# Fewer warming matmuls, a hand-made front order and a split first unit in a spectral-filter and token-mixing kernel

## The chip, the cores and the metric

The kernel runs on one core of one Trainium2 chip. The metric is the device time of one execution in microseconds (us). Beside it stands the span of the profile, from the first to the last instruction, which is shorter: by 1.5 to 1.6 us in every recorded run of the kernel before and of e2, and by 1.75 to 1.9 us in every run of the changed kernel and its other edits. So the changed kernel spends some 0.26 us more outside its span; no run here tells where. "Granted clock" is the share of full speed that TensorE was allowed; it was 0.995 or more in all runs compared below, except where the text says otherwise.

## The reference

A batch of 1 with 2048 tokens of 512 channels is normalized, filtered in the frequency domain, added to itself, normalized again, and mixed along the tokens by a two-layer network.

```python
h  = x + irfft2(rfft2(layernorm(x)) * (w_r + 1j * w_i))   # over tokens and channels
u  = gelu(einsum("bsd,sf->bdf", layernorm(h), w1) + b1)   # F = 1376
h2 = h + transpose(einsum("bdf,fs->bds", u, w2) + b2)
```

Inputs, weights and the output are bf16.

## The kernel before

Every operation is recorded by name (`f2_3_01`, `hh_4`) with the engine it runs on and two numbers in ns: `occ`, how long it keeps its engine, and `lat`, when its result is there. A list scheduler then fixes the order of each engine's program *before anything runs*, always taking the operation that could start first by those numbers. The chip executes each engine's list strictly in that order. So these numbers don't merely describe the program, they shape it.

```python
def act(name, dst, src, func, n, ...):                 # every ScalarE operation
    lat = 186.0 + 0.833 * n + 93.0 * naps + (93.0 if accum is not None else 0.0)
    ...
    return K.op(name, "act", emit, ins=ii, outs=oo, occ=lat - 90.0, lat=lat + 50.0, ...)
...
# schedule(): of all operations that are ready
st = max(eng_free[o.stream], o.dep_ready, avail, o.not_before)
key = (st, -o.prio, o.idx)                             # the smallest key goes next
...
eng_free[e] = st + o.occ
```

The front: 16 tiles of tokens. Statistics of a tile on VectorE (ScalarE for tiles 1 and 3), its reciprocal root on ScalarE, a scaling FS of the transform's matrix, matmuls, an evacuation Y. Some matmuls of zeros ("warming") keep TensorE busy meanwhile.

```python
STAT_ACT = (1, 3)
FS_ENG = {4: "act", 7: "act", 9: "dve", 11: "dve", 13: "dve", 14: "act", 15: "dve"}   # others GpSimd
N_WARM = 20
WARM_AFTER = (4, 3, 2, 1, 1, 0, 1, 0, 0, 0, 0, 0, 0, 0, 0, 0)
```

The middle: 8 units. Per unit two groups of second-transform matmuls (f2, full rows, 256 columns), an evacuation CS for each, cross matmuls (x, on 64 rows each), VectorE's product with the spectral weights, 16 matmuls back (g1, full rows, 128 columns) and an evacuation PQ.

```python
def stage_f2(u):
    for i in range(2):
        G = 2 * u + i
        ...  # 4 matmuls f2_G into one bank
        # CS of G on ScalarE (VectorE for G == 1)
def stage_x(u):
    ...      # 8 matmuls x_2u, x_2u+1 into two banks, half=True (64 rows)
    ...      # one product of 128 x 2048, or two of 1024 for units in V_SPLIT = (0, 7)
def stage_g1(u):
    ...      # twice 8 matmuls and an evacuation PQ on ScalarE
for u in range(8):
    stage_f2(u); stage_x(u); stage_g1(u)
```

After that, per tile: inverse transform (g2, `eo` on ScalarE, g3), the residual on VectorE (`tl`, `th`, `h`), the sum of squares and its root on ScalarE (`q`, `r2`), and the normalized tile on VectorE (`hh`). Each `hh` feeds the first layer of the network on TensorE.

```python
    act(f"eo_{s2}", EO[:, s2, :], lambda bank: ps[:, bank, :], ACT.Copy, 512, ...)
    ...  # tl, th, h on VectorE
    act(f"q_{s2}", junk()[:, :], hs, ACT.Square, 512, ..., accum=V2[:, s2:s2 + 1], prio=9)
    act(f"r2_{s2}", R2[:, s2:s2 + 1], V2[:, s2:s2 + 1], ACT.Abs_reciprocal_sqrt, 1, ...)
    dve(f"hh_{s2}", ...)                               # HH = (h + nm) * r2
```

Of the kernel before, what the change touches and what calls it, by code (L numbers as in the profile page):

```python
# [8 lines left out]
LN_EPS = 1e-5  # L9
# [27 lines left out]
def _row(sign, comp, k2, s):  # L37
    return 4 * (k2 * 2 + s) + 2 * sign + comp
# [52 lines left out]
def build_consts():  # L91
# [22 lines left out]
    fp = fp.reshape(NP, NS2, NP)  # L114
    fp = np.stack([-fp, fp], axis=2)
# [26 lines left out]
    c["E"] = e.reshape(NP, 1024)  # L142
    c["MR"] = np.concatenate([m.reshape(NP, 512), r.reshape(NP, 512)], axis=1)
# [5 lines left out]
PSUM_BANKS = 8  # L149
CELL = 4  # L150
# [28 lines left out]
class Builder:  # L179
    def __init__(self, nc, limits):  # L180
        self.nc = nc
        self.ops = []
        self.writer = {}
        self.readers = {}
        self.tensors = {}
        self.limits = limits
        self.cell_cache = {}

# [37 lines left out]
    def op(self, name, engine, emit, ins=(), outs=(), occ=100.0, lat=None, unit=None, pr=False, pw=False,  # L226
           first=False, last=False, prio=0, nbytes=0, is_dma=False, not_before=0.0, after=(), group=None, rate=DMA_RATE):
# [13 lines left out]
        o.rate = rate  # L241
        deps = {id(d): d for d in after}
# [38 lines left out]
    def schedule(self):  # L281
# [13 lines left out]
        order = []  # L295
        while len(order) < len(ops):
            best = None
            for o in ready:
                bank, avail = None, 0.0
                u = o.unit  # L300
                if u is not None and not u.claimed:
# [5 lines left out]
                    for b in range(PSUM_BANKS - u.nbanks + 1):  # L307
                        if all(bank_unit[i] is None for i in range(b, b + u.nbanks)):
                            t = max(bank_free[b:b + u.nbanks])
                            if cand is None or t < cand[0]:  # L310
                                cand = (t, b)
# [10 lines left out]
            ready.remove(o)  # L322
            o.sched, o.start = True, st
# [11 lines left out]
            if o.is_dma:  # L335
                x0 = max(st + (3200.0 if st < 4000.0 else 1700.0), dma_free)
                dma_free = x0 + o.bytes / o.rate
                o.finish = dma_free + 200.0
            else:
                o.finish = st + o.lat  # L340
# [86 lines left out]
def memory_layout():  # L427
# [26 lines left out]
    add("W", [NP, NG, 2, LW], bf, rw)  # L454
    add("HH", [NP, NS2, D_LEN], bf, rw)
# [28 lines left out]
STAT_ACT = (1, 3)  # L484
RS_GROUPS = ((0,), (2,), (4,), (5,), (6, 7), (8, 9), (10, 11), (12,), (13,), (14,), (15,))
FS_ENG = {4: "act", 7: "act", 9: "dve", 11: "dve", 13: "dve", 14: "act", 15: "dve"}
Y_DVE = ((5, 1), (6, 1), (7, 1))
N_WARM = 20
WARM_AFTER = (4, 3, 2, 1, 1, 0, 1, 0, 0, 0, 0, 0, 0, 0, 0, 0)
V_SPLIT = (0, 7)  # L490
LAST_WARM = 6
# [3 lines left out]
def build_kernel(nc, A_x, A_w_r, A_w_i, B_w1, B_b1, B_w2, B_b2, out):  # L495
# [5 lines left out]
    K = Builder(nc, {"f1": 6, "f2": 2, "x": 2, "g1": 2, "g2": 2, "g3": 2, "mm1": 5, "mm1b": 6, "mm2": 8})  # L501
# [3 lines left out]
    X, FS, Y, CS, V, PQ, EO, H, HH, GT, OUT, W = (T[n] for n in ("X", "FS", "Y", "CS", "V", "PQ", "EO", "H", "HH", "GT", "OUT", "W"))  # L505
# [9 lines left out]
    def dma(name, dst, src, nbytes, stream="sp", outs=(), ins=(), prio=0, strided=False, after=(), group=None, rate=DMA_RATE,  # L515
            not_before=0.0):
        def emit(eng, bank):
            if strided:
                with nc.allow_non_contiguous_dma(reason="small bias gather"):
# [3 lines left out]
                    rate=rate, occ=1000.0 if stream == "pool" else 640.0 if rate < DMA_RATE else 460.0, not_before=not_before)  # L523
# [10 lines left out]
    def act(name, dst, src, func, n, ins=(), outs=None, unit=None, prio=0, last=True, psum=True, bias=None, scale=None, accum=None):  # L534
# [15 lines left out]
        return K.op(name, "act", emit, ins=ii, outs=oo, occ=lat - 90.0, lat=lat + 50.0, unit=unit, pr=unit is not None,  # L550
# [13 lines left out]
    def ldf(q, pr_, stream="sp", nb=0.0):  # L564
        sl = slice(4 * q, 4 * q + 4)
        dma(f"ld_FP{q}", FP[:, sl, :, :], cin[f"FP{q}"][:, :, :, :], 1 << 18, outs=[FP[:, sl, :, :]], prio=pr_, stream=stream, not_before=nb)

    for q, (a, b) in enumerate(((0, 2), (2, 4), (4, 6), (6, 8), (8, 12))):
        ldx(a, b, 90 - q)
    ldf(2, 84)  # L570
    ldx(12, 16, 83)
    ldf(3, 82)
    ldf(0, 90, "act")
    act("table", T["tb"][:, 0:1], EPS[:, 0:1], ACT.Abs_reciprocal_sqrt, 1, ins=[EPS[:, 0:1]], prio=88)
    ldf(1, 87, "act", 1800.0)
    dma("ld_E", EM[:, 0:1024], cin["E"][:, :], 1 << 18, outs=[EM[:, 0:1024]], prio=44)
    dma("ld_MR", EM[:, 1024:2048], cin["MR"][:, :], 1 << 18, outs=[EM[:, 1024:2048]], prio=43)
    wload = {}
    for ch, (u0, u1) in enumerate(((0, 1), (1, 4), (4, 8))):
        g0, ng = 4 * u0, 4 * (u1 - u0)  # L580
        lst = []
        for w, dram in ((0, A_w_r), (1, A_w_i)):
            for comp in range(2):
                d = W[comp::4, g0:g0 + ng, w, :]
                lst.append(dma(f"ld_wp{ch}_{w}{comp}", d, bass.AP(dram.tensor, g0 * LW, [[64 * LW, 32], [LW, ng], [1, LW]]),
                               32 * ng * 514, prio=42 - ch, group=f"w{ch}", rate=300.0))
                h0, nh = (g0, ng) if g0 else (1, ng - 1)
                d = W[2 + comp::4, h0:h0 + nh, w, :]
                lst.append(dma(f"ld_wm{ch}_{w}{comp}", d, bass.AP(dram.tensor, (64 - h0) * LW, [[64 * LW, 32], [-LW, nh], [1, LW]]),
                               32 * nh * 514, prio=42 - ch, group=f"w{ch}", rate=300.0))  # L590
                if g0 == 0:
                    d = W[2 + comp::4, 0, w, :]
                    lst.append(dma(f"ld_wz{ch}_{w}{comp}", d, bass.AP(dram.tensor, 32 * LW, [[64 * LW, 32], [1, LW]]),
                                   32 * 514, prio=42 - ch, group=f"w{ch}", rate=300.0))
        for u in range(u0, u1):
            wload[u] = lst
    dma("ld_D2", EM[:, 2048:3072], cin["D2"][:, :], 1 << 18, outs=[EM[:, 2048:3072]], prio=30)
    dma("ld_IF", IF[:], cin["IF"][:, :, :], 1 << 19, outs=[IF[:]], prio=29)
    w1src = B_w1.rearrange("(p s2) f -> p s2 f", s2=NS2)
    for q in range(4):  # L600
        sl = slice(4 * q, 4 * q + 4)
        dma(f"ld_w1_{q}", W1[:, sl, :], w1src[:, sl, :], 4 * F_LEN * 2 * NP, outs=[W1[:, sl, :]], prio=28 - q, after=wload[7][-1:])
# [13 lines left out]
    ZT, BV = T["ZT"], T["bv"]  # L616
    K.op("zt", "dve", lambda eng, bank: eng.memset(ZT[:, :], 0.0), outs=[ZT[:, :]], occ=200.0, prio=60)  # L617
# [9 lines left out]
    def fs_op(i):  # L627
        e = FS_ENG.get(i, "pool")
        rs = RS[:, i:i + 1]
        if e == "act":  # L630
            act(f"fs{i}", FS[:, i, :, :], FP[:, i, :, :], ACT.Copy, 256, ins=[FP[:, i, :, :]], scale=rs, prio=30)
        else:
            dve(f"fs{i}", lambda eng, bank: eng.tensor_scalar(FS[:, i, :, :], FP[:, i, :, :], rs, None, op0=ALU.mult),  # L633
                [FP[:, i, :, :], rs], [FS[:, i, :, :]], 120, prio=30, engine=e, lat=920.0 if e == "pool" else None)

    def stat_act(i):
# [3 lines left out]
        nm = NM[:, i:i + 1]  # L640
        dve(f"nm_{i}", lambda eng, bank: eng.tensor_scalar(nm, SM[:, i:i + 1], -1.0 / D_LEN, None, op0=ALU.mult), [SM[:, i:i + 1]], [nm], 1, prio=33, engine="pool", lat=210.0)
        dve(f"bv_{i}", lambda eng, bank: eng.tensor_scalar(BV[:, i:i + 1], nm, nm, LN_EPS, op0=ALU.mult, op1=ALU.subtract), [nm], [BV[:, i:i + 1]], 1, prio=33, engine="pool", lat=210.0)
        act(f"rs_{i}", RS[:, i:i + 1], V1[:, i:i + 1], ACT.Abs_reciprocal_sqrt, 1, ins=[V1[:, i:i + 1]], bias=BV[:, i:i + 1],
            scale=-1.0 / D_LEN, prio=32)
        fs_op(i)

    def stat_dve(grp):
        a, b = grp[0], grp[-1] + 1
        for i in grp:
# [3 lines left out]
            dve(f"st_{i}", lambda eng, bank, i=i, x=x: eng.bn_stats(ST[:, i, 0:6], x), [x], [ST[:, i, 0:6]], 512, prio=25)  # L653
# [15 lines left out]
    Yv = Y[:].rearrange("p b y g (n k) -> p b (y g) n k", k=4)  # L669
    for q in range(8):  # L670
        for b in range(2):
            unit = PsumUnit("f1", 1)
            lastmm = {}
            for n in range(2):
                n2 = 2 * q + n
                lo = X[:, n2, b * NP:b * NP + NP]
                hi = X[:, n2, 256 + b * NP:256 + b * NP + NP]
                f = FS[:, n2, 1, :]
                f2 = bass.AP(f.tensor, f.offset, [list(f.ap[0]), [0, 2], [1, NP]])
                fm = FS[:, n2, :, :]  # L680

                def o(bank, n=n):
                    return ps[:, bank, n * 256:n * 256 + 256]
                mm(f"f1_{n2}_{b}a", o, lo, f2, unit, True, False, n == 0, 14, 256, ins=[lo, f])
                lastmm[n] = mm(f"f1_{n2}_{b}b", o, hi, fm, unit, False, True, False, 14, 256)

            def src(bank):
                v = ps[:, bank, :].rearrange("p (n g k) -> p n g k", n=2, k=4)
                return v.rearrange("p n g k -> p g n k")
            dst = Yv[:, b, :, 2 * q:2 * q + 2, :]  # L690
            if (q, b) in Y_DVE:
                dve(f"y_{q}_{b}", lambda eng, bank, dst=dst, src=src: eng.tensor_copy(dst, src(bank)), [], [dst], 512, unit=unit, prio=28)
            else:
                act(f"y_{q}_{b}", dst, src, ACT.Copy, 512, unit=unit, prio=28)
            for n in range(2):
                for w_ in range(WARM_AFTER[2 * q + n] if b == 1 else 0):
                    warm(f"warmf{q}{n}{w_}", wu, 13, after=[lastmm[n]], last=2 * q + n == LAST_WARM)

    cs_ops = {}

    def stage_f2(u):
        for i in range(2):
            G = 2 * u + i
            unit = PsumUnit("f2", 1)
            for par in range(2):
                for b in range(2):
                    mm(f"f2_{G}_{par}{b}", lambda bank, par=par: ps[:, bank, par * 256:par * 256 + 256],
                       Y[:, b, par, 2 * G:2 * G + 2, :].rearrange("p g k -> p (g k)"), E[:, b, par, :],
                       unit, b == 0, b == 1, par == 0 and b == 0, 10, 256)
            dst = CS[:, G, :, :, :].rearrange("p y c j -> p (y c j)")  # L710
            if G == 1:
# [169 lines left out]
```

## Time and profile before

| | before |
|---|---|
| first three runs | 133.78, 165.66, 187.84 us |
| span of the profile, granted clock | 132.4 us, 1.00 |
| busy: matmul, weight load, VectorE, ScalarE | 93%, 56%, 52%, 48% |
| last evacuation Y of the first transform | 18.93 us |
| first and last product with the weights | 21.48 to 39.36 us |
| first add after the inverse transform | 42.63 us |

Shares over the whole span say little: four stages follow one another, each with another engine as its limit. The prediction reads them in turn. It shows none of the following three answers, and they turned out to matter. The first is TensorE's timeline early in the middle (start, length, engine, line, operation, output<-inputs, shape, count, and what ended an idle time before it); the next line is from the stage table for 18 to 36 us (stretch, length, then busy us and instructions of matmul, weight load, VectorE, ScalarE, GpSimd, then clock, DMA share and GB/s).

```profile
18.62 2.18 PE L531 MATMUL ps<-EM,Y 128*128 128x256 bf16 x17 [0.41 <-ACT Y L549]
20.73 0.61 PE L531 MATMUL ps<-CS,EM 64*128 64x256 bf16 x8
21.28 0.61 PE L531 MATMUL ps<-EM,Y 128*128 128x256 bf16 x4
```
```profile
18.00:36.00 18.00, 17.40 (x218) 13.12 (x218) 15.90 (x10) 14.07 (x28) 1.22 (x7) 1.00 1.07 305
```

TensorE does not pause between these groups. It has 17 f2 matmuls done before the first cross matmul, a stock for the units to come. The third answer is VectorE's timeline from the first product on:

```profile
21.48 17.88 DVE L739 TENSOR_TENSOR V<-ps,W 128x1024 bf16<-128x1024 f32 x10 [0.94 <-PE ps L531]
42.63 0.42 DVE L790 TENSOR_TENSOR TT<-ps,X 128x256 f32<-128x256 f32 x1 [3.27 <-PE ps L531]
```

Ten products in a row without a single wait: before the change VectorE set the pace here.

### The profile page before, as it was taken

How to read it: one execution, taken by the hardware profiler on the slowest of the kernel's cores; microseconds unless marked ns; L12 is line 12 of the kernel's file. 1: busy time of each engine (PE TensorE's matmuls, PEld its weight loads, DVE VectorE, ACT ScalarE, POOL GpSimd, SP SyncE). 2: the span in 40 equal slices, each digit the busy share in tenths (PEclk: the TensorE clock that was granted, in tenths of full speed). 3: DMA queues.
4: the chain of work that ended last, by engine and by line, in shares of the span. 5: the costliest groups of instructions: out<-in, count | busy, mean ns of one | idle time of the engine just before them, and what ended most of it. 6: DMA issues, size and time to landing. Idle time of an engine off the chain costs nothing.

```text
span 132.4 us, 2013 instructions
## 1 busy us (share of the span) xinstructions
PE 123.7 (93%) x776; PEld 74.5 (56%) x786; DVE 69.3 (52%) x127; ACT 63.3 (48%) x146; POOL 12.4 (9%) x33
## 2 busy tenths in 40 slices
PE   6989989999977979999999999999999999999990
PEld 2436656788666736544434444456666666666660
DVE  0499867999981999999960000000242332423322
ACT  4579976978966999986689322222000000000000
POOL 0199920000300000000000000000000000000000
PEclk9999999999999999999999999999999999999999
DMA  2999699999999999992000000000111112111121
GB/s 80 375 396 364 153 244 273 286 322 283 419 426 417 410 408 411 417 295 74 0 0 0 0 0 0 5 0 0 40 40 70 49 40 82 42 57 62 40 79 40
DMA packets 16648, 22.16 MB, mean 167 GB/s; under 512 B 2720, under 2 KB 12960, under 8 KB 16128
## 3 DMA queue, kind: packets, MB, share of 16 engines
q1 hardware_dynamic: 16352, 21.52, 47.5%
q10 hardware_dynamic: 288, 0.52, 1.1%
q8 instruction: 6, 0.10, 0.3%
q14 instruction: 2, 0.02, 0.0%
HBM read 19.95 MB, written 2.10 MB: 167 GB/s over the span
## 4 chain that ended last, share of the span: by engine, by line
PE 51%; DVE 32%; ACT 9%; DMA 3%; POOL 2%; issue 1%; DVEq 0%; ACTq 0%
PE ps L531 50%; DVE V L739 13%; DVE H L799 7%; ACT Y L549 5%; DVE TT L790 4%; DVE TT L792 4%; DVE HH L804 4%; DMA X<-in_A_x_dram 3%; POOL FS L633 1%; ACT rs L549 1%; ACT FS L549 1%; ACT JK L549 1%; DVE OUT L829 1%; ACT PQ L549 0%; PE ps L621 0%
## 5 line engine op out<-in xcount | busy, mean ns | idle before, releaser
L531 PE MATMUL ps<-HH,W 128*128 128x512 bf16 (+1 forms) x173 | 40.3, 379 | 1.3 <-DVE HH L804 0.9
L531 PE MATMUL ps<-GT,W 128*128 128x512 bf16 (+1 forms) x172 | 37.9, 379 | 0.2
L829 DVE SCALAR_TENSOR_TENSOR OUT<-ps,B2f,H 128x512 bf16<-128x512 f32 x16 | 12.0, 750 | 48.7 <-PE ps L531 48.7
L531 PEld LDWEIGHTS ps<-GT,W 128*128 128x128 bf16 (+1 forms) x176 | 25.3, 144 | 12.8
L531 PEld LDWEIGHTS ps<-HH,W 128*128 128x128 bf16 (+1 forms) x176 | 17.2, 100 | 21.2 <-DVE HH L804 1.9
L739 DVE TENSOR_TENSOR V<-ps,W 128x2048 bf16<-128x2048 f32 (+1 forms) x10 | 17.9, 1856 | 0.9 <-PE ps L531 0.9
L549 ACT ACTIVATE GT<-ps,B1f 128x512 bf16<-128x512 f32 (+1 forms) x11 | 7.1, 689 | 14.6 <-PE ps L531 14.6
L549 ACT ACTIVATE JK<-H,nm 128x512 bf16<-128x512 bf16 x16 | 11.6, 722 | 3.0 <-DVE H L799 2.9
L653 DVE BATCH_NORM_STATS2 st<-X 128x6 f32<-128x512 bf16 x14 | 9.2, 669 | 4.1 <-DMA X<-in_A_x_dram 4.1
L621 PE MATMUL ps<-ZT 128*128 128x512 bf16 x32 | 9.6, 434 | 1.6 <-DVE ZT L617 1.2
L799 DVE TENSOR_TENSOR H<-ps,TT 128x512 bf16<-128x512 f32 x16 | 10.9, 682 | 0.0
L549 ACT ACTIVATE PQ<-ps 128x512 bf16<-128x512 f32 x16 | 8.9, 602 | 3.5 <-PE ps L531 3.3
L531 PE MATMUL ps<-EM,PQ 128*128 128x256 bf16 x64 | 9.0, 273 | 0.8 <-ACT PQ L549 0.7
L531 PE MATMUL ps<-EM,V 128*128 128x128 bf16 x128 | 9.2, 219 | 0.5 <-DVE V L739 0.5
L549 ACT ACTIVATE EO<-ps 128x512 bf16<-128x512 f32 x16 | 9.2, 596 | 0.9 <-PE ps L531 0.9
L549 ACT ACTIVATE CS<-ps 128x512 bf16<-128x512 f32 x15 | 8.3, 607 | 2.1 <-PE ps L531 2.1
L531 PE MATMUL ps<-EM,Y 128*128 128x256 bf16 x64 | 8.7, 273 | 0.4 <-ACT Y L549 0.4
L531 PE MATMUL ps<-FS,X 128*128 128x256 bf16 x64 | 8.4, 274 | 0.5 <-POOL FS L633 0.4
L531 PEld LDWEIGHTS ps<-EM,V 128*128 128x128 bf16 x128 | 7.5, 98 | 2.3 <-issue 1.4
L633 POOL TENSOR_SCALAR FS<-FP,rs 128x256 bf16<-128x256 bf16 x9 | 8.6, 965 | 0.6 <-ACT rs L549 0.5
L790 DVE TENSOR_TENSOR TT<-ps,X 128x256 f32<-128x256 f32 x16 | 6.7, 417 | 3.3 <-PE ps L531 3.3
L531 PEld LDWEIGHTS ps<-EM,PQ 128*128 128x128 bf16 x64 | 6.2, 98 | 2.9 <-ACT PQ L549 0.9
(36 smaller groups left out, 79.1 us busy)
## 6 DMA issues: line engine op xcount, KB each, us to landing
W<-in_B_w_dram SPq DMA_DIRECT2D x4, 1376.0 KB, 11.7
W<-in_B_w_dram SPq DMA_DIRECT2D x10, 512.0 KB, 18.3
out_dram<-OUT SPq DMA_DIRECT2D x16, 128.0 KB, 1.7
W<-in_A_w_r_dram SPq DMA_DIRECT2D x4, 257.0 KB, 4.5
W<-in_A_w_i_dram SPq DMA_DIRECT2D x4, 257.0 KB, 5.0
X<-in_A_x_dram SPq DMA_DIRECT2D x4, 256.0 KB, 5.0
X<-in_A_x_dram SPq DMA_DIRECT2D x2, 512.0 KB, 6.6
W<-in_A_w_r_dram SPq DMA_DIRECT2D x4, 192.8 KB, 3.3
```

The costliest lines, as they stand in the source:

```text
L531: return K.op(name, "pe", lambda eng, bank: eng.matmul(outf(bank), lhsT, rhs, start=start, stop=stop), ins=ins or [lhsT, rhs], occ=occ, la ...
L549: return eng.activation(dst, s, func, **kw)
L621: return K.op(name, "pe", lambda eng, bank: eng.matmul(ps[:, bank, :], ZT[:, 0:NP], ZT[:, :], start=True, stop=True), ins=[ZT[:, :]], occ= ...
L633: dve(f"fs{i}", lambda eng, bank: eng.tensor_scalar(FS[:, i, :, :], FP[:, i, :, :], rs, None, op0=ALU.mult), [FP[:, i, :, :], rs], [FS[:, ...
L653: dve(f"st_{i}", lambda eng, bank, i=i, x=x: eng.bn_stats(ST[:, i, 0:6], x), [x], [ST[:, i, 0:6]], 512, prio=25)
L739: return eng.tensor_tensor(vout, s, win, ALU.mult)
L790: dve(f"tl_{s2}", lambda eng, bank, tt=tt, xl=xl: eng.tensor_tensor(tt[:, 0, :], ps[:, bank, 256:512], xl, ALU.add), [xl], [tt[:, 0, :]], ...
L792: dve(f"th_{s2}", lambda eng, bank, tt=tt, xh=xh: eng.tensor_tensor(tt[:, 1, :], xh, ps[:, bank, 256:512], ALU.subtract), [xh], [tt[:, 1, ...
L799: return eng.tensor_tensor(hs.rearrange("p (h d) -> p h d", h=2), e, tt[:, :, :], ALU.add)
L804: dve(f"hh_{s2}", lambda eng, bank, s2=s2, hs=hs: eng.tensor_scalar(HH[:, s2, :], hs, NM[:, s2:s2 + 1], R2[:, s2:s2 + 1], op0=ALU.add, op1 ...
L829: dve(f"fin{s2}", lambda eng, bank, dst=dst, bia=bia, hs=hs: eng.scalar_tensor_tensor(dst, ps[:, bank, :], bia, hs, op0=ALU.add, op1=ALU.add),
```

## The change

It is meant to shorten the front and the latency behind it. Fewer warming matmuls run up front, and two of them wait for the first statistics. Tile 1's statistics move to VectorE, tile 0's and 3's scaling to ScalarE; tile 3 alone stays on ScalarE. The order of VectorE, ScalarE, GpSimd and TensorE in the front is written out by hand. The first unit of the middle is split into half-size steps shared by two engines, and so is the last evacuation PQ. Loads are regrouped.

```diff
-STAT_ACT = (1, 3)
+STAT_ACT = (3,)
-FS_ENG = {4: "act", 7: "act", 9: "dve", 11: "dve", 13: "dve", 14: "act", 15: "dve"}
+FS_ENG = {0: "act", 3: "act", 7: "act", 9: "dve", 11: "dve", 13: "dve", 14: "dve", 15: "dve"}
+FRONT = {"dve": """bn_0 ag_0 bn_1 ag_1 bn_2 bn_4 ...""", "act": ..., "pool": ..., "pe": ...}
-N_WARM = 20
-WARM_AFTER = (4, 3, 2, 1, 1, 0, 1, 0, 0, 0, 0, 0, 0, 0, 0, 0)
+N_WARM = 9
+N_GATED = 2                     # after bn_0, the first statistics
+WARM_AFTER = (3, 2, 0, 1, 1, 0, 0, 1, 0, 0, 0, 0, 0, 0, 0, 0)
+    K.forced = {e: FRONT[e].split() for e in ("dve", "act", "pool")}
...
@@ def act
-                    occ=lat - 90.0, lat=lat + 50.0, ...
+                    occ=lat - 120.0, lat=lat + 50.0, ...
...
@@ stage_f2, stage_x
+            split = u == 0      # a unit of PSUM per half; CS half on ScalarE, half on VectorE
+            if u == 0:          # cross matmuls and two 512-column products per group, from W0
...
@@ stage_g1
+            split = (u, h) == (7, 1)     # PQ: first half on VectorE, second on ScalarE
```

The line in `act` is one number in a diff of several hundred lines. The diff also gives each tile its own evacuation Y, restricts which PSUM banks the middle's groups may use, and changes the scheduler's numbers for DMA; none of these three was tested alone.

> **What bounds the kernel now.** I read the chain of waits first, then the table of stages, then the groups by form, then the timeline of the front. All times are from the one profiled execution, 132.4 us at full clock (133.9 us as timed). Two of the three unprofiled runs took 165.66 and 187.84 us, the third 133.78. The fast profile cannot explain the slow two, so I predict the fast state only, from 133.8 us.
>
> The chain, in order of time, cut to its turning points:
> ```profile
> 0.72 4.15 DMA X<-in_A_x_dram
> 4.89 1.34 ACT JK L549 x4
> ...
> 17.10 1.47 ACT Y L549 x3
> 18.57 0.05 issue
> 18.62 2.77 PE ps L531 x25
> ...
> 21.48 1.04 DVE V L739
> ...
> 22.62 15.62 DVE V L739 x8
> 38.24 0.14 issue
> ...
> 40.13 0.61 ACT PQ L549
> ...
> 42.63 0.42 DVE TT L790
> ...
> 68.05 8.81 PE ps L531 x40
> ```
> Four limits follow one another. To 18.6 us ScalarE sets the pace (statistics, then evacuations Y of the first transform). To 21.5 it is latency: matmul, evacuation CS, matmul. To about 39 VectorE multiplies by the spectral weights with no gap. From 42.6 to 68 VectorE adds and normalizes, then TensorE runs dense to 129.2. Everything after 42.6 us is untouched by the change, so what is won before is carried to the end.
>
> The stage table (columns: stretch, length, busy us and instructions of matmul, weight load, VectorE, ScalarE, GpSimd, clock, DMA share, GB/s) confirms who is full:
> ```profile
> 10.00:15.00 5.00, 4.95 (x38) 3.39 (x38) 4.72 (x17) 4.97 (x14) 4.59 (x5) 1.00 0.85 271
> 22.00:30.00 8.00, 8.00 (x108) 6.33 (x105) 8.00 (x5) 6.28 (x13) 0.00 (x0) 1.00 1.12 307
> ```
> In the front ScalarE is full (4.97 of 5), and VectorE and GpSimd nearly so: work can only be traded among three loaded engines. In the middle VectorE is 8.00 of 8.00. The matmul figure is not a limit: it counts pipelined durations and, in the front, warming filler.
>
> **What the Trainium skill says.** (1) "TensorE: Matmul & The Clock Gate", Part 1: a cold array starts 512-column matmuls 426.7 ns apart, a warm one 215.7; it warms after about 3.4 us of activity in a free-running window. The timeline agrees: the warming weight loads start at 1.57, 2.00, 2.43 ... 4.13 us, 0.43 apart, then twelve take 2.47 us, 0.21 each. The array became warm near 4.1 us, 3 us after the first matmul. (2) "ScalarE: Activation LUTs", What ACT_TABLE_LOAD costs: 186 ns + 0.833 ns per element, 93 more per pointer operand, and back-to-back instructions overlap by about 93. At 512 that is 612 ns; Y shows 607. At 256 columns without a pointer it is 399. (3) "VectorE: DVE Perf Modes", The TRN2 errata: an fp32 tensor_tensor takes (N+151)/0.96 ns. At 1024 and 2048 that gives 1224 and 2291; the weight products show 1218 and 2281. (4) "PSUM — Partial Sum Buffer", PSUM bank collisions: two engines must not touch one bank and quadrant at once. Splitting an evacuation between ScalarE and VectorE therefore needs separate banks, which the diff gives; no run here shows a collision.
>
> **The change, part by part.** The groups that price it:
> ```profile
> L739 DVE TENSOR_TENSOR V<-ps,W 128x1024 bf16<-128x1024 f32 x4 | 4.7, 1218 | 0.9 <-PE ps L531 0.9
> L653 DVE BATCH_NORM_STATS2 st<-X 128x6 f32<-128x512 bf16 x14 | 9.2, 669 | 4.1 <-DMA X<-in_A_x_dram 4.1
> L549 ACT ACTIVATE JK<-X 128x512 bf16<-128x512 bf16 x4 | 2.5, 617 | 2.3 <-DMA X<-in_A_x_dram 2.3
> L549 ACT ACTIVATE Y<-ps 128x512 bf16<-128x512 f32 x13 | 7.0, 607 | 0.0
> ```
> *Fewer warming matmuls.* 20 up front become 9, plus 2 released by the first VectorE statistics; fillers between first-transform groups fall from 12 to 8. The first 9 cold ones last 9 x 0.43 = 3.9 us, so to 5.0; the gated two start near 5.6. This removes no work from the path: in the chain the front hangs on ScalarE. Worth 0, with a risk given below.
>
> *Front order.* ScalarE before: 4 statistic passes at 0.71 (4.89 to 7.73) = 2.84, 13 reciprocal roots at 0.18 = 2.34, 3 scalings at 0.45 = 1.35, 13 evacuations at 0.49 (x2 take 0.97 in the chain) = 6.37: 12.9 us. Starting at 4.89 that gives 17.8; measured 18.57, so about 0.8 us were waits (0.60 of it one wait for GpSimd's bias at 9.15). After: 2 passes 1.42, 12 roots 2.16, 3 scalings 1.35, 13 full evacuations 6.37, and tile 15 in two halves at about 0.28 (estimate: 0.40 less the overlap) 0.56: 11.9 us. But it now starts only when the first VectorE statistics are done: 4.89 + 0.70 + 0.18 and a hop, 5.85. 5.85 + 11.9 = 17.7; I allow 0.4 for waits: **18.1**. VectorE: 15 tiles at 0.66 start to start (8.13, 8.79, 9.45 in the timeline) = 9.9 from 4.9; tile 1 now fills a 0.32 us wait for the second transfer, so the added tile costs only about half. With two scalings inside at 0.27 the statistics end near 15.8; the last roots come 0.3 later, three scalings to 16.9, evacuations 12 and 14 (0.65 each) to 18.1. Both engines meet at 18.1. Before, ScalarE's last Y ended 18.57 and VectorE's at 18.93 (18.24 + 0.69). GpSimd makes 8 scalings instead of 9 and is no longer last. Gain 0.5 to 0.85 us.
>
> *Split first middle unit.* Before: second-stage matmuls from 18.62, held for VectorE's Y to 18.99; CS starts at 19.53 and 19.86, 0.6 and 0.69 long; the cross matmuls wait for both, start at 20.73; first product at 21.48, thus 2.49 us after the last Y landed. After: from 18.1, two matmuls 0.22 and 0.2 drain for a half bank; ScalarE and VectorE copy one 256-column half each, second one from 18.8 for 0.4: 19.2; four half-row cross matmuls and drain, 0.4; first product near **19.7**. That is 1.75 earlier, the front's part included. The price: unit 0 makes four 512-column products instead of two of 1024. Pitch is 1.15 at 1024 (21.48, 22.62) and 2.2 at 2048, so 0.62 at 512 (estimate): 4 x 0.62 - 2 x 1.15 = +0.2.
>
> *Loads.* Spectral weights of unit 0 come in 8 transfers instead of 12, so the issuing queue saves 4 x 0.65 = 2.6 us for every later weight transfer. Bytes stay. Worth 0 by itself, but it pays for products moving 1.7 us earlier.
>
> *Last g1 half split.* Before: last product ends 39.36, PQ 40.13 to 40.74. After, VectorE copies the first group while the last is made, and ScalarE copies only 256 columns: 0.40 instead of 0.61, so -0.2.
>
> Sum: -1.75 + 0.2 - 0.2 = -1.75; I round to -1.8. 133.8 - 1.8 = **132.0 us**, 1.3% less.
>
> **The rivals.** *ScalarE holds the front.* Its sum is only an estimate with 0.4 us of waits; if hand order makes it wait as before (0.8) and Y ends at 18.5, the time is 132.4. For: it starts 0.96 us later than before. Against: 1 us less work. *The clock opens late.* The window is free-running. With 20 warmers the array could not stop working before it was warm; with 9 and a hole at 5.0 to 5.6 it may stay cold until 8 to 10 us. For: this trace opened at 4.1, only 0.9 us before the nine would end. Against: cold first-transform matmuls take 0.21 each, 0.85 a tile, about the rate at which the scaled tiles arrive anyway. Cost 0 to 1.5 us: 132 to 133.5. *Weights come late.* The DMA share is above 1.00 from 22 us on and unit 4's weights were last issued at 24.7 and needed near 30.4, with about 5 us from issue to landing. If DMA throughput rather than issue sets the landing, products stall and 1 us returns: 133. Against: the share was only 0.57 at 14 to 16 us, so the queue did have room. *More is won.* If the new order also closes the small holes of the middle (0.66 ScalarE waits at 36.8 and similar), the end moves 2.7 us or more: 131. Against: VectorE was already full there. A gain vanishing after 42.6 us I hold unlikely: the same work follows, VectorE and TensorE run out together at 68.
>
> **Range and chances.** Central 132.0. My walk has an error of about 0.7 us in the front and 0.4 in the first unit. Low 130.4 is a front at 17.5 with the middle also better; high 134.0 is a cold front and late weights together, plus timing noise. Faster by over 2% means below 131.1, 0.9 us better than the sum: 0.2. Slower by over 2% needs a broken front and is hard to reach: 0.04. The rest, 0.76, is within 2%.
>
> **What would show it.** In the changed trace: Y ends near 18.1 (before 18.93); first product near 19.7 (21.48); products end near 37.7 (39.36) with VectorE full from first to last; the first add after the transforms near 40.9 (42.63); from there to the end the same 89.8 us as before. ScalarE's first root near 5.85, its front work near 12 us. Warming weight loads still change from 0.43 to 0.21 apart before 5.5 us; if they or the first-transform matmuls stay at twice their pitch beyond 8 us, the clock rival holds. A VectorE wait for DMA among the products shows the weights rival. The prediction is wrong if the first product comes after 20.5 us, or if the time from it to the end is not about 111 us.

## The result and the profile after

| | before | changed |
|---|---|---|
| median us | 149.8 of 4 (133.78, 133.94, 165.66, 187.84) | 133.88 of 4 (133.81 to 133.96) |
| ratio of the fast runs, 95% interval | | 1.0002 (0.9978 to 1.0026) |
| span of the profile | 132.36 | 132.17 |

A ratio is the mean time of one kernel's fast runs over that of the other's fast runs of the same rounds, so it is not quite the ratio of the medians quoted. The two slow runs of before did not return in 34 later ones, which took 133.57 to 135.08 us on three chips. They stay unexplained; 149.8 is no basis for a comparison, and the change did not remove them as far as anything here shows.

So nothing was gained. The small lead that the trace shows at the end (0.15 us, below) is smaller than the 0.26 us that the changed kernel spends more outside its span. But the first product did start earlier. Because the input's landing itself moves from run to run (4.59 to 4.94 us), all later tables count from that landing, the start of the first statistics. They give, in us: the end of the last Y; the first product; the start of unit 1's first product; the end of the last product; the first add after the inverse transform; the last normalized tile HH; the last output step. The two profiles of the changed kernel agree in these distances to 0.01.

| from landing | Y end | first product | unit 1 | products end | first add | last HH | end |
|---|---|---|---|---|---|---|---|
| before | 14.04 | 16.59 | 18.86 | 34.47 | 37.74 | 64.41 | 125.08 |
| changed | 13.45 | 15.23 | 17.95 | 33.83 | 36.96 | 64.25 | 124.93 |
| changed, taken again (e5) | 13.46 | 15.24 | 17.96 | 33.84 | 36.97 | 64.26 | 124.94 |
| lead over before | 0.59 | 1.36 | 0.91 | 0.64 | 0.78 | 0.16 | 0.15 |

The lead is 1.36 us at the first product. It melts to 0.64 by the last product, and to 0.16 by the last HH. Two stages gave it back, and the second of them is one that the change was not thought to touch.

VectorE's timeline of the changed kernel, at the places of those shown for before:

```profile
19.95 2.48 DVE L813 TENSOR_TENSOR V<-ps,W 128x512 bf16<-128x512 f32 x4 [0.32 <-PE ps L553]
22.67 15.88 DVE L828 TENSOR_TENSOR V<-ps,W 128x2048 bf16<-128x2048 f32 x8 [0.24 <-PE ps L553]
...
41.68 0.42 DVE L894 TENSOR_TENSOR TT<-ps,X 128x256 f32<-128x256 f32 x1 [2.08 <-PE ps L553]
```

VectorE, which never waited among the products, now waits for TensorE ahead of unit 1 (0.24 at 22.67). The chain of waits (start, length, engine, what, line, count) and the stage row show how far this went:

```profile
16.79 1.21 DVE Y L744 x2
18.14 13.51 PE ps L553 x163
31.67 4.50 DVE V L828 x2
```
```profile
18.00:36.00 18.00, 17.85 (x224) 13.65 (x224) 16.55 (x12) 13.99 (x29) 1.27 (x7) 1.00 1.08 303
```

Before, the chain stood on VectorE for 15.62 us from 22.62 on. Now it stands on TensorE from 18.14 to 31.65, 163 matmuls, and reaches VectorE only for the last two products. The matmul time rose from 17.40 to 17.85 of 18 us. TensorE's timeline lists no idle time from 18.14 to 37.57, and it begins differently from before:

```profile
18.14 1.35 PE L553 MATMUL ps<-EM,Y 128*128 128x256 bf16 x10 [0.44 <-DVE Y L744]
19.43 0.39 PE L553 MATMUL ps<-CS,EM 64*128 64x256 bf16 x4
```

The first cross matmuls come after 10 f2 matmuls instead of 17, so the stock of f2 results is smaller when VectorE begins.

### The profile page after: what moved, and what is told of

It reads as the page before. It is cut to its first block, busy times and chain, and to the rows that moved or that the text cites. A ratio compares the mean times of both kernels' runs of the same rounds, so it can differ in the third digit from the quotient of the medians.

```text
span 132.2 us, 2004 instructions
## 1 busy us (share of the span) xinstructions
PE 123.3 (93%) x773; PEld 73.2 (55%) x773; DVE 70.5 (53%) x133; ACT 62.7 (47%) x144; POOL 10.7 (8%) x30
## 3 DMA queue, kind: packets, MB, share of 16 engines
HBM read 19.95 MB, written 2.10 MB: 167 GB/s over the span
## 4 chain that ended last, share of the span: by engine, by line
PE 60%; ACT 16%; DVE 16%; DMA 3%; issue 3%
PE ps L553 60%; ACT JK L571 5%; ACT Y L571 4%; DVE H L903 4%; DVE V L828 3%; DMA X<-in_A_x_dram 3%; ACT EO L571 3%; DVE HH L908 2%; ACT rs L571 2%; DVE TT L894 2%; DVE TT L896 2%; ACT r L571 2%; ACT FS L571 1%; DVE Y L744 1%; ACT PQ L571 1%
## 5 line engine op out<-in xcount | busy, mean ns | idle before, releaser
L553 PE MATMUL ps<-HH,W 128*128 128x512 bf16 (+1 forms) x176 | 41.0, 379 | 1.3 <-DVE HH L908 1.1
L828 DVE TENSOR_TENSOR V<-ps,W 128x2048 bf16<-128x2048 f32 (+1 forms) x8 | 15.7, 2017 | 0.4 <-PE ps L553 0.2
L682 DVE BATCH_NORM_STATS2 st<-X 128x6 f32<-128x512 bf16 x15 | 9.8, 665 | 3.6 <-DMA X<-in_A_x_dram 3.6
L571 ACT ACTIVATE PQ<-ps 128x512 bf16<-128x512 f32 (+1 forms) x16 | 9.1, 591 | 3.7 <-PE ps L553 3.6
L648 PE MATMUL ps<-ZT 128*128 128x512 bf16 x21 | 7.6, 481 | 2.1 <-DVE ZT L591 1.2
L571 ACT ACTIVATE CS<-ps 128x512 bf16<-128x512 f32 (+1 forms) x16 | 8.4, 577 | 1.6 <-PE ps L553 1.6
L571 ACT ACTIVATE Y<-ps 128x512 bf16<-128x512 f32 (+1 forms) x15 | 7.9, 566 | 0.2 <-PE ps L553 0.2
L660 POOL TENSOR_SCALAR FS<-FP,rs 128x256 bf16<-128x256 bf16 x8 | 7.4, 937 | 6.7 <-ACT rs L571 6.4
```

What stands on the lines that cost most here:

```text
L553: return K.op(name, "pe", lambda eng, bank: eng.matmul(outf(bank), lhsT, rhs, start=start, stop=stop), ins=ins or [lhsT, rhs], occ=occ, la ...
L571: return eng.activation(dst, s, func, **kw)
L648: return K.op(name, "pe", lambda eng, bank: eng.matmul(ps[:, bank, :], ZT[:, 0:NP], ZT[:, :], start=True, stop=True), ins=[ZT[:, :]], occ= ...
L660: dve(f"fs_{i}", lambda eng, bank: eng.tensor_scalar(FS[:, i, :, :], FP[:, i, :, :], rs, None, op0=ALU.mult), [FP[:, i, :, :], rs], [FS[:, ...
L682: dve(f"bn_{i}", lambda eng, bank, i=i, x=x: eng.bn_stats(ST[:, i, 0:6], x), [x], [ST[:, i, 0:6]], 512, prio=25)
L828: return eng.tensor_tensor(vout, s, win, ALU.mult)
```

## The experiments

Three theories were on the table. **A:** the loss after the products comes from the scheduler constant, which changes the order of the normalizing stage. **B:** the loss among the products comes from the order of f2 and x matmuls, which lets unit 1's product wait. **C:** it comes from TensorE being full in that stage, so that any order only moves the wait. The rival to A is that the new data flow itself (split PQ, other bank use) costs the time there.

All kernels but e2 are edits of the changed kernel; from e3 on, except e5, e13 and e14, they carry e1's edit too, so their base is e1. No kernel differs from before by the 2% at which a verdict of faster or slower is given; the readings below rest on the distances in the traces, with the times beside them.

### e1: the scheduler constant back

```diff
-        ... occ=lat - 120.0, lat=lat + 50.0, ...
+        ... occ=lat - 90.0, lat=lat + 50.0, ...
```

> The changed kernel with one number undone: the ScalarE occupancy that its own scheduler assumes is latency minus 90 ns again, not minus 120. From the first sum after the transforms on, the program order of VectorE, ScalarE and TensorE is then that of the kernel before, instruction by instruction. Theory A (the order lost it): the stretch from that first sum to the dense matmuls falls from 26.05 us to 25.4 (before: 25.4), no VectorE wait for the second root before 67 us, and the time is 0.6 us under the changed kernel: 133.3. Rival B (the earlier stage meets loads or a slower ScalarE, whatever the order): the stretch stays near 26.0 and the time at 133.9.

Measured: 133.25 us (133.15 to 133.54, 6 runs) against 134.05 of before; ratio 0.9937 (0.991 to 0.9963). From first add to last HH it took 26.67 us, as before, where the changed kernel took 27.29; the end came 0.68 earlier than in the changed kernel. After the transforms the program order of VectorE, ScalarE and TensorE is now that of before.

How an order costs time can be read from two pairs of lines. First the changed kernel: ScalarE from the root r of tile 2 to that of tile 3, then VectorE's normalized tile 3:

```profile
47.73 0.29 ACT L571 ACTIVATE r<-v,eps 128x1 f32<-128x1 f32 x1
47.91 0.59 ACT L571 ACTIVATE EO<-ps 128x512 bf16<-128x512 f32 x1
48.39 0.73 ACT L571 ACTIVATE JK<-H,nm 128x512 bf16<-128x512 bf16 x1
...
49.09 0.60 ACT L571 ACTIVATE EO<-ps 128x512 bf16<-128x512 f32 x1
49.57 0.30 ACT L571 ACTIVATE r<-v,eps 128x1 f32<-128x1 f32 x1
```
```profile
49.41 0.41 DVE L896 TENSOR_TENSOR TT<-X,ps 128x256 f32<-128x256 bf16 x1
49.91 0.41 DVE L908 TENSOR_SCALAR HH<-H,nm,r 128x512 bf16<-128x512 bf16 x1
```

Then the same for e1:

```profile
47.53 0.30 ACT L571 ACTIVATE r<-v,eps 128x1 f32<-128x1 f32 x1
47.72 0.72 ACT L571 ACTIVATE JK<-H,nm 128x512 bf16<-128x512 bf16 x1
...
48.43 0.59 ACT L571 ACTIVATE EO<-ps 128x512 bf16<-128x512 f32 x1
48.90 0.30 ACT L571 ACTIVATE r<-v,eps 128x1 f32<-128x1 f32 x1
```
```profile
49.13 0.41 DVE L896 TENSOR_TENSOR TT<-X,ps 128x256 f32<-128x256 bf16 x1
49.45 0.41 DVE L908 TENSOR_SCALAR HH<-H,nm,r 128x512 bf16<-128x512 bf16 x1
```

Between the two roots the changed kernel makes two evacuations EO, e1 one. Root to root takes 1.84 us instead of 1.37. The root of tile 3 ends at 49.87 in the changed kernel, and its HH starts 0.50 after the TT before it instead of 0.32. The profile prints no idle time there: HH starts only 0.09 after TT ends, and the list names idle stretches above 0.15. But an instruction that need not wait starts about 0.08 us *before* its predecessor ends, so the delay is the sum of both, 0.17. It is a wait for the root, since HH starts 0.04 after the root's end. Six HH of the changed kernel start so: 0.11, 0.17, 0.11, 0.21, 0.10 and 0.03 us later than after the same predecessor elsewhere, 0.73 in all. In e1 two such delays are left, of 0.02 and 0.06. The difference, 0.65, accounts for the 0.62 that the stage lost. Theory A holds for the changed kernel. e1 also beats both kernels.

### e2: the same constant in the kernel before

```diff
-        ... occ=lat - 90.0, ...      (kernel before)
+        ... occ=lat - 120.0, ...
```

> The mirror: the kernel before with only that number changed to 120. Its order after the transforms is then that of the changed kernel. Theory A: the same stretch grows from 25.4 to about 26.0 us, with VectorE waits of 0.1 to 0.2 us for the second root, and the time is about 134.4, 0.5 to 0.6 over before (part may be offset if its middle order also moves). Rival B: stretch 25.4 and time 133.8.

Measured: 136.04 us, ratio 1.0143 (1.0115 to 1.0171). First add to last HH: 27.30 instead of 26.67, the 0.63 that A expects, in a kernel without any other part of the change; after the transforms its trace shows the changed kernel's order on all three engines. The new data flow is ruled out as the cause of this loss. The total is a miss, 2.06 at the end rather than about 0.6: the constant also reordered the front (Y ended 0.85 later) and put a 0.48 us wait among the products. The changed kernel has its front pinned by hand, so the constant could not reorder it there.

### e3, e4, e8: the split, and two orders of TensorE

e3 makes the first unit whole again:

```diff
-            split = u == 0
+            split = False               # CS of 512 on ScalarE and VectorE,
...                                      # two products of 1024 from W0
```

> As e1, but with the first middle unit whole again: one 512-wide evacuation on ScalarE and one on VectorE, two products of 1024 instead of four of 512. Order after the transforms as before. My theory: the first product comes about 1.1 us later than in e1 (near 21.0), unit 1's product only 0.7 later because four small products cost 0.2 more and then wait 0.24, so the time is 0.6 to 0.8 over e1. Rival (the split is repaid wholly inside the product stage): equal times.

e4 keeps the split and lists TensorE's order by hand, with f2_3 ahead of x_1; e8 also moves the next unit's cross matmuls up:

```diff
+    ... f2_2_10 f2_2_11 f2_3_00 ... f2_3_11 x_1_00 ...         # e4
-    ... f2_5_00 ... f2_6_00 x_2_00 ... x_3_11 g1_0_00 ...      # e8, on top of e4
+    ... x_2_00 ... x_3_11 f2_5_00 ... f2_6_00 g1_0_00 ...
```

> As e1, with one swap in TensorE's order: the second transform of group 3 ahead of the cross matmuls of group 1, so that ScalarE's evacuations 2 and 3 follow each other. Theory: the 0.24 us wait of VectorE ahead of unit 1's product goes, later products move with it, time 0.2 under e1: about 133.1. Rival (TensorE is as full as VectorE in this stage): the wait only moves to a later product and the time equals e1.

> e4 with the cross matmuls of unit 1 also ahead of the second transforms of groups 5 and 6. Theory C (TensorE is full from the second transform to 35.5 us and sets the pace of the products): VectorE's wait of 0.23 us ahead of unit 1 goes, but an equal wait appears at a later unit, and the last product ends within 0.15 us of e1, counted from the landing of the first input (33.77). Rival D (only this order made VectorE wait): the last product ends 0.3 us sooner.

| from landing | first product | unit 1 | products end | end | us | ratio |
|---|---|---|---|---|---|---|
| e1 (split) | 15.25 | 17.97 | 33.77 | 124.25 | 133.25 | 0.9937 |
| e3 (whole) | 16.13 | 18.40 | 33.93 | 124.42 | 133.62 | 0.9972 |
| e4 | 15.24 | 17.95 | 33.75 | 124.24 | 133.43 | 0.9960 |
| e8 | 15.24 | 17.64 | 33.91 | 124.39 | 133.40 | 0.9934 |

The split brings the first product 0.88 forward, unit 1 by 0.43, the last product by 0.16 and the end by 0.17. I had expected 0.6 to 0.8 to stay. As timed the difference is 0.37, but the two intervals overlap. e4 changes nothing: x_2 still stands behind f2_4 to f2_6. e8 does remove the wait at unit 1, but look at VectorE's products in e1 and then in e8:

```profile
22.56 8.88 DVE L828 TENSOR_TENSOR V<-ps,W 128x2048 bf16<-128x2048 f32 x4 [0.23 <-PE ps L553]
31.61 6.75 DVE L828 TENSOR_TENSOR V<-ps,W 128x2048 bf16<-128x2048 f32 x4 [0.16 <-PE ps L553]
```
```profile
22.30 4.48 DVE L848 TENSOR_TENSOR V<-ps,W 128x2048 bf16<-128x2048 f32 x2
26.93 4.61 DVE L848 TENSOR_TENSOR V<-ps,W 128x2048 bf16<-128x2048 f32 x2 [0.16 <-PE ps L573]
31.82 6.75 DVE L848 TENSOR_TENSOR V<-ps,W 128x2048 bf16<-128x2048 f32 x4 [0.28 <-PE ps L573]
```

The wait has moved to 26.93 and 31.82, and the products end no sooner than in e1. B falls. The order decides where VectorE waits, hardly how long.

### e9, e10, e12: less work for TensorE

These give wrong results on purpose (relative error 0.02): half of the g1 matmuls is left out, which shortens TensorE's work and touches nothing that a product reads.

```diff
-                    for w in range(2):
+                    for w in range(1):      # start and stop both True
```

e9 does it to e1, e10 to e3 (whole unit), e12 to e8.

> Wrong results on purpose: e1 with the first inverse transform (g1) done for one of its two weight parts, 64 of 128 matmuls left out, about 3.6 us of TensorE's work in the middle; VectorE's products are all still made. Theory C (TensorE sets the pace of the products): with the relief VectorE waits for nothing after the first product, products take about 17.9 us from first start to last end (e1: 18.52), and the last product ends 0.6 to 0.8 us sooner than in e10, counted from the landing of the first input. Rival D (ScalarE's evacuations or the four small products themselves cost it): products still take 18.4 us or more, lead over e10 0.2.

> Wrong results on purpose: e3 (first unit whole) with the same 64 g1 matmuls left out. Products from first start to last end 17.8 us as in e3, no waits; only the distance to e9 matters.

> Wrong results on purpose: e8's order (cross matmuls early) with 64 of 128 g1 matmuls left out, so that TensorE has room from the start of the stage, which e9's order did not give it. Theory C (TensorE's queue sets the pace of the products): VectorE waits for nothing after its first product, products take 17.95 to 18.05 us in all (e1 18.52, e8 18.68, e9 18.43), and the last ends near 33.25 after the landing of the first input (e10: 33.93). Rival D (something else makes it wait): waits of 0.2 us or more remain and the last product ends at 33.6 or later.

| products end, from landing | all g1 | half of g1 |
|---|---|---|
| first unit whole (e3, e10) | 33.93 | 33.93 |
| split, x ahead of f2 (e8, e12) | 33.91 | 33.29 |
| split, the scheduler's order (e1, e9) | 33.77 | 33.69 |

e9 settled nothing. With fewer g1 matmuls the scheduler itself pulled later f2 matmuls ahead of the cross matmuls, and from 18.99 TensorE again ran without a hole above 0.1 us to 29.2; its time is not used either, as the granted clock was 0.974 and 0.987 in its two runs. That is why e12 fixes the order. e12 is a single run (132.44 us, state unknown), so its timeline counts here more than its time. e10's clock was 0.987 as well, in its one fast run. The missing clock lies late in the stage (0.50 from 36 to 40 us in e9, 0.83 and 0.82 from 30 to 36 and 36 to 40 in e10), where VectorE waits for nothing in either, so it does not move the end of the products.

e12's VectorE:

```profile
19.94 2.48 DVE L828 TENSOR_TENSOR V<-ps,W 128x512 bf16<-128x512 f32 x4 [0.32 <-PE ps L568]
22.34 15.64 DVE L843 TENSOR_TENSOR V<-ps,W 128x2048 bf16<-128x2048 f32 x8
```
```profile
18.00:36.00 18.00, 16.29 (x180) 11.03 (x181) 16.90 (x13) 14.24 (x29) 1.27 (x7) 1.00 1.06 298
```

All waits after the first product are gone, and 0.64 of the 0.88 us of lead over e10 is kept at the last product. With a whole unit, halving g1 moved nothing: there VectorE is the limit. With the split and all of g1, TensorE is. Theory C holds. A rival would be that fewer g1 matmuls free PSUM banks sooner; but TensorE was hardly waiting for banks or anything else, for between 19 and 35 us e8, with all of g1, has a single hole above 0.1 us, of 0.15.

The arithmetic behind it, from the start times in the trace of before: f2 matmuls start 0.109 apart, cross matmuls 0.0545 (64-row halves run side by side), g1 matmuls 0.056. Each block of eight cross matmuls costs another 0.20 or so at the change to 64 rows and back: its first starts 0.10 later after an f2 than another f2 would, and the next group starts 0.55 after that first, where 8 x 0.0545 is 0.44. That is 64 x 0.109 + 64 x 0.0545 + 128 x 0.056 + 8 x 0.20 = 19.2 us. From the first f2 (18.14) to the last g1 (39.4, where the last PQ starts) the changed kernel has 21.3 us, and the split adds a ninth change of rows: an estimate of 19.4 us of work. The products need 17.9. So TensorE had more work than VectorE all along. In both kernels its starts follow each other without a hole above 0.15 us from 19 to 35 us, although in the kernel before VectorE never waited: even starts show a full engine, not yet which engine the other waits for. By this count what hid TensorE's work was its head start: before the first product it worked 2.86 us (18.62 to 21.48) in the kernel before and 1.81 (18.14 to 19.95) in the changed one. The split gave VectorE an earlier start, but took it out of TensorE's.

### e6, e7, e11: the other parts

```diff
-N_WARM = 9                    # e6
-N_GATED = 2
+N_WARM = 20
+N_GATED = 0                   # and before's WARM_AFTER and LAST_WARM
...
-    K.forced = {...}          # e7
+    K.forced = {}
...
-            split = (u, h) == (7, 1)      # e11
+            split = False
```

> e1 with the warming of the kernel before: 20 up front, none gated, 12 fillers. My prediction said that the fewer warmers are worth 0: time equal to e1 within 0.2 us, first product at the same distance from the landing of the first input (15.25 us). Rival: the 20 hold TensorE until 7.1 us, the first transforms (ready near 6.5) start late and up to 0.5 us returns.

> e1 with the hand-made front order taken out (the scheduler orders the front itself; the assignment of tiles to engines stays). The kernel's own cost model puts the second transform 0.27 us later, but it does not know the chip. My theory: the front ends 0.3 to 0.6 us later, and as everything after it is full, the whole of it shows in the time: 133.6 to 133.9. Rival: the middle has slack, time equal to e1.

> e1 with the split of the last g1 half undone (one evacuation of 512 columns on ScalarE). My prediction put the split at 0.2 us: the last product to the first sum grows from 3.13 to 3.3 us and the time by 0.15 to 0.2 us. Rival: no difference.

e6: 133.51 us, ratio 0.9961 (0.9929 to 0.9994). The front ends 0.31 later than in e1, and the end comes 0.30 later. TensorE at the start, first of the changed kernel, then of e6:

```profile
5.47 0.60 PE L648 MATMUL ps<-ZT 128*128 128x512 bf16 x2 [0.46 <-DVE st L682]
6.56 0.61 PE L553 MATMUL ps<-FS,X 128*128 128x256 bf16 x4 [0.48 <-ACT FS L571]
```
```profile
3.28 4.38 PE L648 MATMUL ps<-ZT 128*128 128x512 bf16 x15
7.49 1.04 PE L553 MATMUL ps<-FS,X 128*128 128x256 bf16 x8
```

Two 512-column matmuls in 0.60 us at 5.47: the clock is already warm with nine. With twenty, the queue is occupied to 7.66, and the first real matmul starts at 7.49 instead of 6.56.

e7: 135.4 us, ratio 1.0081 (1.0038 to 1.0124), with Y ending 2.75 us later than in e1 and the end 2.75 later. I had expected 0.3 to 0.6. But the profiled run is one of three with a granted clock of 0.986 or 0.987, and the clock was missing in the front. The stage table from 8 to 10 us, first of e7, then of e1 (the clock is the third number from the end):

```profile
8.00:10.00 2.00, 2.00 (x8) 0.89 (x7) 2.00 (x7) 2.00 (x7) 1.07 (x3) 0.50 1.02 398
```
```profile
8.00:10.00 2.00, 1.92 (x14) 0.89 (x11) 2.00 (x7) 1.96 (x7) 1.77 (x2) 1.00 0.98 381
```

Before that, TensorE had stood idle for 0.65 us ahead of 5.45 and for 0.98 ahead of 7.04. The three runs at the lower clock have spans of 134.1 to 134.4, the other three, at 0.998 or more, 132.8 to 133.0, and e1's are 131.4 to 131.7. So about 1.4 of the 2.75 us (an estimate from these spans) is the scheduler's own front, slower than the author's list, and the rest is half clock in the front. This is close to the prediction's clock rival, met without the hand-made order. A shift of the whole front reaches the end undiminished in e6 and e7, since it moves TensorE's start along with VectorE's.

e11: 133.44 us, ratio 0.9959 (0.994 to 0.9978). Last product to first add takes 3.35 instead of 3.13 us; the end comes 0.20 later. The split of the last PQ is worth 0.2.

### e5, e13, e14: the changed kernel again, and one order at a time

e5 is the changed kernel unaltered. e13 keeps the constant at 120 and forces VectorE's order after the transforms to before's, ScalarE's to the changed kernel's; e14 does the reverse.

```diff
+TAIL = {"dve": """tl_0 th_0 tl_1 h_0 th_1 tl_2 h_1 ... h_2 hh_0 ...""", "act": ...}
+    for e in ("dve", "act"):
+        K.forced[e] += TAIL[e].split()
```

> The changed kernel itself, on the chip of the next three, as their base. Both theories: within 0.3% of the kernel before, 133.8 to 134.1 us, and 0.6 us over e1.

> The changed kernel (its 120 ns constant kept) with only VectorE's program order after the transforms set to that of the kernel before; ScalarE's order there stays as changed (TensorE's follows the scheduler). From the waits seen: VectorE's order alone explains the waits for the roots of tiles 0, 6 and 7 (0.11, 0.2, 0.1), ScalarE's those of tiles 3 and 4 (0.17, 0.11). Expected: first sum to last normalized tile 26.95 us, between 27.29 (changed) and 26.67 (before); time 133.6.

> The mirror of e13: only ScalarE's order after the transforms set to that of the kernel before, VectorE's as changed. Expected by the same reading: stretch about 26.95 to 27.0 us, time 133.6. If ScalarE's order is the whole cause: 26.67 here and 27.29 in e13.

e5: 133.94 us against 134.25, ratio 0.9978 (0.9954 to 1.0002); its points are in the table of the result. e13: 133.87, ratio 0.9972 (0.9944 to 0.9999). e14: 133.97, ratio 0.9971 (0.994 to 1.0003). Both take 27.19 us from first add to last HH, where I had expected 26.95: each order alone wins back 0.10 of the 0.62. VectorE in e13, then in e14:

```profile
49.91 0.41 DVE L918 TENSOR_SCALAR HH<-H,nm,r 128x512 bf16<-128x512 bf16 x1 [0.19 <-ACT r L581]
```
```profile
56.14 0.41 DVE L918 TENSOR_SCALAR HH<-H,nm,r 128x512 bf16<-128x512 bf16 x1 [0.36 <-ACT r L581]
```

In both VectorE still waits for a root of ScalarE, at other tiles. So neither order alone explains the loss. That it is the match between the lists that counts is argued from these waits; e1 restores all of them at once. Both lists together with TensorE's left as changed, and TensorE's alone, were not tried.

## Why the prediction was right or wrong

The predicted time, 132.0 us, missed by 1.9; the range (130.4 to 134.0) held 133.88 near its upper edge, and "within 2%" was right. But the forecast gain of 1.8 us did not come: it was 0.15 at the end of the trace, and none as timed. The terms of the sum:

| term | predicted | measured, from landing |
|---|---|---|
| front, end of Y | -0.83 | -0.59 |
| Y end to first product | -0.92 | -0.77 |
| product stage | +0.2 | +0.72 |
| last product to first add | -0.2 | -0.14 |
| after the first add | 0 | +0.62 |
| sum | -1.75 | -0.16 |

The extra 0.26 us outside the span stand beside this sum; no term of the prediction covers them.

**Right.** The mechanism of the front: Y ended at 18.17 (predicted 18.1), and the first product came at 19.95 (19.7). Both look closer than they are, since the input landed 0.17 earlier: from landing they came 0.24 and 0.42 later than forecast. ScalarE's first root started at 5.67 (5.85), 0.95 after landing (0.96). The clock did not open late, no product waited for weights, and the split of PQ had its size (0.2 in e11). One of the prediction's own signs of being wrong came true: from the first product to the end it took 112.2 us (110.9 before), not about 111.

**Wrong, first step: "The matmul figure is not a limit: it counts pipelined durations".** I set aside a busy time of 8.00 of 8 us (17.40 of 18 over the stage) because of what the column may hide, and did not replace it by a count. Start-to-start times give 19.2 us of TensorE work for a stage I called VectorE's. The +0.2 for the finer products was about right (0.13: 2.40 instead of 2.27 us up to unit 1, in e8 and e12, which don't wait there). The rest of the +0.72 is waiting for TensorE: 0.32 ahead of unit 1 (2.72 less 2.40) and 0.27 later. So the lead that the split gives at the first product (0.88 in e3) bought almost nothing, as e3 measured directly (0.17 at the end) and e12 explains.

**Wrong, second step: "Everything after 42.6 us is untouched by the change".** Its data flow is untouched, its program is not. The diff held the line with 120 for 90, and I passed over it, since it moves no instruction by itself. The scheduler did. "From there to the end the same 89.8 us" measured 90.5 in the changed kernel and 89.9 in e1. This is the larger of the two, 0.62 of the 1.59 missing in one line, and a gain vanishing there was the rival that I held unlikely.

**Smaller: "Fewer warming matmuls ... Worth 0".** They are worth 0.3 us, since matmuls in a queue are not only harmless filler: real ones stand behind them (e6). The front's gain thus contains this 0.3. Why the front fell 0.24 short of the forecast was not tested, but the trace shows the term: ScalarE's twelve roots took 0.21 us each from start to start (0.18 in the sum) and its thirteen full Y 0.50 each (0.49), while its waits were 0.23 (0.4 allowed).

What also stays open is the slow runs of before, which no later run showed.

## What to carry to other kernels

Before calling an engine free, add up its work by start-to-start times and compare it with the stage; if it is nearly full, a head start that another engine gets by splitting its first step will be waited away, while an earlier start for both is kept. Where a list scheduler writes the programs, a cost constant is part of the change: compare the order of every engine in every stage, not only where the edit points. Engines that hand work to each other had to be reordered together here; one list alone returned a sixth of what all of them did.

## What the Trainium skill lacked or had wrong

- "Perfetto Trace Analysis", Identifying the Most-Contended Engine, calls matmul busy time no good measure of the distance to roofline, because pipelined instructions look smaller in the trace, and points to the share of peak matmul work and to weight-load busy instead. Here the weight-load row alone would mislead: it showed 13.65 of 18 us, while the matmul row was at 17.85 of 18 and TensorE was the limit. The page has no count of an engine's work from start-to-start times, which gave 19.4 us against 17.9 for VectorE.
- "TensorE: Matmul & The Clock Gate", Back-to-back issue gap, gives about 81 ns per matmul at 128 columns and 131 at 512 as sustained figures with a weight load each. These runs show 56 ns at 128 columns and 216 at 512 (median from start to start of the dense stage that ends the changed kernel) in streams with a weight load each; the page's formula for a single matmul, N/2.4 + 2.5 ns, fits both, and the 109 ns at 256.
- No page has the time that a change between 128-row and 64-row matmuls costs; "TensorEngine Tiling (Array Packing)", Key Properties, only says that changing the tiling mode drains TensorE. Here it was about 0.20 us for each block of eight cross matmuls, 1.6 us in this kernel.
- No page says that a wait first uses up the overlap of two VectorE instructions before it shows as idle time: HH starts 0.08 us before its predecessor ends when it need not wait and 0.04 after the end of ScalarE's root when it does, so a delay of 0.17 us left 0.09 of idle time, and one of 0.11 left 0.03.
